# Summing the linear state over two token tiles in PSUM, and issuing it inside a value burst

## The chip, the cores and the metric

One core of one Trainium2 chip runs the whole program. The metric is device time in microseconds of that core; lower is better. Repeated runs of one kernel here spread over 0.5 to 2 us (0.1 to 0.4%), and the change is worth about as much or less, so most of this study reads stretches of the trace and not whole times.

## The reference, cut to what matters

Two attention blocks over the same x (2048 tokens, 1024 wide, 32 heads of 32) are mixed by a gate per token. Block A is linear attention, block B a local one with 8 positions at a dilation of 2.

```python
# block A
phi = lambda t: jnp.where(t > 0, t + 1, jnp.exp(t)) + 1e-6
pq, pk = phi(q), phi(k)
kv = jnp.einsum("bhsd,bhse->bhde", pk, v)      # the linear state
z  = jnp.einsum("bhsd->bhd", pk)               # its denominator part
num = jnp.einsum("bhqd,bhde->bhqe", pq, kv)
den = jnp.einsum("bhqd,bhd->bhq", pq, z)[..., None] + 1e-6
a = (num / den) @ wo_A
# block B: softmax over 8 earlier positions, times V, @ wo_B
g = sigmoid((x * gate_w).sum(-1, keepdims=True))
out = g * a + (1 - g) * b
```

## The kernel before

The program is a list of operations with reads and writes. A list scheduler in the kernel's own build step orders them for each engine by estimated times, and emits semaphore waits. TensorE does dense projections (128x512 matmuls in groups of 8, 1.73 us a group), and between them three kinds of short bursts of small matmuls: scores (S) and values (PV) of the local part, and the linear state (kv), one burst for each of 16 token tiles. A column of ones beside V (in az, the moving operand; pk is the stationary one) gives z as a 33rd column.

```python
vr = Ring([... "v%d" % i ... for i in range(3)])     # V of the local part, three deep
pk = Ring([... for i in range(2)])                   # phi(k) of a token tile
az = Ring([... for i in range(2)])                   # V of a token tile and ones
# ... cut ...
            def values():
                def each(e):        # 64 matmuls, 57 rows x 33 columns, 64x64 tiles
                    # ... cut ...
                P.op("pe", each, 0.55, mode="c", reads=[vt.all(), E.all()], writes=[s.iv for s in SO], name="PV")
                # ... cut: reciprocal and product on VectorE, store ...
# ... cut ...
        def slot(rate):             # called once for each dense group
            slot_n[0] += 1
            while later and later[0][0] <= slot_n[0]:
                later.pop(0)[1]()
            while states and states[0][0] <= slot_n[0]:
                states.pop(0)[1]()
            # ... cut ...
        def state(t, pkt, azt):
            bank = main.next()

            def fn(e):
                last = None
                for s in range(8):
                    for c in range(4):
                        h = 16 * (s // 4) + 4 * c + s % 4
                        last = e.matmul(bank.ap()[32 * c:32 * c + 32, s * 33:s * 33 + 33], pkt[:, h * 32:(h + 1) * 32], azt[:, h, :],
                                        start=True, stop=True, tile_position=(0, 32 * c))
                return last
            P.op("pe", fn, 0.22, mode="c", reads=[pkt.all(), azt.all()], writes=[bank.iv], name="kv")
            # VectorE: kva = bank (first tile) or kva + bank
# ... cut ...
                if r == 3:
                    states.append((slot_n[0] + 4, lambda t=t, pkt=pkt, azt=azt: state(t, pkt, azt)))
                slot(FILL)
# after the last tile, on VectorE: kvb and kvT (the state, transposed, for fold),
# and 16 small copies of z for the denominator:
        for c in range(4):
            for r in range(4):
                k = 4 * (c % 2) + r
                P.op("dve", lambda e, ...: e.tensor_copy(zsel[32 * r:32 * r + 32, c:8:4, k:k + 1], kva[32 * c:32 * c + 32, r:8:4, 32:33]), 0.1, ...)
# fold(): 16 matmuls of 32 rows x 512 into four banks: the state times wo_A, four times
# over(u): 8 matmuls for the denominators of 512 tokens (den), Ln and Exp on ScalarE,
#   then out to HBM and back as a broadcast (rc_hbm, rb), then 8 products on VectorE:
            for c in range(4):
                P.op("sp", ...dma_start(rc_hbm[...], R[...]), 0.5, ..., lat=0.5)
            # ... cut ...
                P.op("dve", lambda e, B=B, dst=dst: e.tensor_tensor(dst, dst, B[:, :], ALU.mult), 0.65, reads=[reg, B.all()], writes=[reg])
```

Of the kernel before, what the change touches and what calls it, by code (L numbers as in the profile page):

```python
# [7 lines left out]
ALU = mybir.AluOpType  # L8
AX = mybir.AxisListType
BF16 = mybir.dt.bfloat16  # L10
F32 = mybir.dt.float32
# [3 lines left out]
H = 32  # L15
# [1100 lines left out]
def build_kernel(nc, A_x, A_wqkv, A_wo, B_x, B_wqkv, B_wo, gate_w, out):  # L1116
# [67 lines left out]
    qd = Ring([SB([128, 8, 2, 114], BF16, "qd%d" % i, at=pq0.lo + 4096 * i) for i in range(2)])  # L1184
    par = SB([128, 2], F32, "par")
    eps = SB([128, 1], F32, "eps")
    gwb = SB([128, 1024], BF16, "gwb")
    gt = SB([128, NT], F32, "gt")
    g = SB([128, NT], F32, "g")
    gm = SB([128, NT], F32, "gm")  # L1190
# [2 lines left out]
    kva = SB([128, 8, 33], F32, "kva")  # L1193
    mx4 = SB([128, 4], F32, "mx4")
    mx1 = SB([1, 4], F32, "mx1")
    flag = SB([1, 1], I32, "flag")
    warm = SB([128, 512], BF16, "warm")
    er = Ring([SB([128, 512], BF16, "e%d" % i) for i in range(3)])

    ph = base[0]  # L1200
# [3 lines left out]
    Er = Ring([SB([128, 32 * 57], BF16, "E%d" % i) for i in range(2)])  # L1204
    ot = Ring([SB([128, 1024], BF16, "ot%d" % i) for i in range(2)])
    rs = Ring([SB([128, 16], F32, "rs%d" % i) for i in range(4)])
    vr = Ring([SB([128, 33 * H], BF16, "v%d" % i) for i in range(3)])
    mtmp = [SB([128, 2, 57], BF16, "mt%d" % i, at=vr.t[2].lo + 256 * i) for i in range(2)]
    base[0] = max(base[0], top_)
    kvT = SB([128, 256], BF16, "kvT")  # L1210
    RAr = Ring([SB([128, 512], F32, "ra%d" % i, at=t.lo) for i, t in enumerate((Er.t[0], Er.t[1]))])
    RBr = Ring([SB([128, 512], F32, "rb%d" % i, at=kT.lo + 2048 * i) for i in range(12)])
    mxr = SB([1, 4, 128], F32, "mxr", at=vr.t[2].lo)

    ph = base[0]
    mx = [SB([128, 1024], BF16, "mx%d" % i, at=ph + 2048 * i) for i in range(2)]
    pk = Ring([SB([128, 1024], BF16, "pk%d" % i) for i in range(2)])
    az = Ring([SB([128, H, 33], BF16, "az%d" % i) for i in range(2)])
    xn = Ring([SB([128, 1024], BF16, "xn%d" % i, at=az.t[i].lo) for i in range(2)])
    top_ = base[0]  # L1220
    base[0] = ph
# [12 lines left out]
    dps = lambda n: 0.14 + n / 960.0  # L1234

    def plan(seen):

        P = Prog(nc, nc.alloc_semaphore)
# [167 lines left out]
        SO = banks[4:8]  # L1406
# [37 lines left out]
        def rest(e_, qs, nq, t0, k0, m, vt, Q, s_fn):  # L1444
            P.op("pe", s_fn, 0.46, mode="r", reads=[kT.part((0, 8), (t0 + k0[0], t0 + k0[1] + 64)), Q.all()], writes=[s.iv for s in SO], name="S")
            E, _ = Er.next()
            P.op("act", lambda e: e.activation(E[:, 0:32 * nq].rearrange("p (j q) -> p j q", j=4), ps[:, 4:8, 0:8 * nq], ACT.Exp), act(32 * nq),  # L1447
                 reads=[s.iv for s in SO], writes=[E.all()])
            ev = lambda: E[:, 0:32 * nq].rearrange("p (g q) -> p g q", g=16)
            P.op("dve", lambda e: e.tensor_tensor(ev(), ev(), m[:, :, :].rearrange("p r q -> p (r q)")[:, None, :].to_broadcast([128, 16, 2 * nq]), ALU.mult),  # L1450
                 0.15 + 32 * nq / 1920.0, reads=[E.all(), m.all()], writes=[E.all()])

            def values():

                def each(e):
                    for i in range(16):
                        for w in range(2):
                            hd = 16 * w + i
                            for h in range(2):
                                c = 33 * (i % 8)  # L1460
                                g_ = place(hd)
                                last = e.matmul(SO[2 * h + i // 8].ap(c, c + 33)[64 * w:64 * w + nq, :], E[64 * h:64 * h + 64, g_ * nq:(g_ + 1) * nq],  # L1462
                                                vt[64 * h:64 * h + 64, hd * 33:hd * 33 + 33], start=True, stop=True, tile_position=(64 * h, 64 * w))
                    return last
                P.op("pe", each, 0.55, mode="c", reads=[vt.all(), E.all()], writes=[s.iv for s in SO], name="PV")
                o, os_ = ot.next()
                for h in range(2):
                    r, _ = rs.next()
                    bv = lambda h=h: ps[:, 4 + 2 * h:6 + 2 * h, 0:264].rearrange("p k (i c) -> p k i c", c=33)
                    two = [SO[2 * h].iv, SO[2 * h + 1].iv]  # L1470
                    P.op("dve", lambda e, r=r, bv=bv: e.reciprocal(r[:, :].rearrange("p (k i) -> p k i", k=2), bv()[:, :, :, 32:33].rearrange("p k i c -> p k (i c)")), 0.2,  # L1471
                         reads=two, writes=[r.all()])
                    P.op("dve", lambda e, r=r, bv=bv, h=h: e.tensor_tensor(  # L1473
                        o[:, 512 * h:512 * h + 512].rearrange("p (k i c) -> p k i c", k=2, c=32), bv()[:, :, :, 0:32],
                        r[:, :].rearrange("p (k i) -> p k i", k=2)[:, :, :, None].to_broadcast([128, 2, 8, 32]), ALU.mult), dps(512),
                        reads=two + [r.all()], writes=[o.part((512 * h, 512 * h + 512))])
                q0 = t0 + qs
                for w, (r0, r1) in [(w, r_) for w in range(2) for r_ in ((0, 48), (48, nq))]:
                    P.op("sp", lambda e, w=w, r0=r0, r1=r1: e.dma_start(
                        oB_hbm[q0:q0 + 2 * nq, 512 * w:512 * w + 512].rearrange("(h q) f -> q h f", h=2)[r0:r1], o[64 * w + r0:64 * w + r1, :].rearrange("p (h f) -> p h f", h=2)), 0.5,  # L1480
                        reads=[o.all()], writes=[[("O%d_%d" % (w, r0), q0, q0 + 2 * nq, None)]], chan="oo%d_%d_%d" % (os_, w, r0), lat=0.3)
                while rows[0] < NT and q0 + 2 * nq >= 128 * (rows[0] + 1):
                    t, rows[0] = rows[0], rows[0] + 1
                    P.op("sp", lambda e, t=t: e.dma_start_transpose(qT[:, :, t * 128:(t + 1) * 128], oB_hbm[t * 128:(t + 1) * 128, :]), 1.5,
                         reads=[[("O%d_%d" % (w, r0), t * 128, (t + 1) * 128, None)] for w in range(2) for r0 in (0, 48)], writes=[qT.part((0, 8), (t * 128, (t + 1) * 128))], chan="ot%d" % t, lat=1.3)
            after(PVLAG, values)
# [6 lines left out]
        def slot(rate):  # L1493
            slot_n[0] += 1
            while later and later[0][0] <= slot_n[0]:
                later.pop(0)[1]()
            while states and states[0][0] <= slot_n[0]:
                states.pop(0)[1]()
            pace[0] = min(pace[0] + rate, 1.0) if todo else 0.0
            if todo and pace[0] >= 1.0:  # L1500
                pace[0] -= 1.0
                fill(*todo.pop(0))
# [33 lines left out]
        for z in az.t:  # L1536
            P.op("pool", lambda e, z=z: e.memset(z[:, :, 32:33], 1.0), 0.2, writes=[z.part((0, H), (32, 33))])

        def state(t, pkt, azt):
            bank = main.next()  # L1540

            def fn(e):
                last = None
                for s in range(8):
                    for c in range(4):
                        h = 16 * (s // 4) + 4 * c + s % 4
                        last = e.matmul(bank.ap()[32 * c:32 * c + 32, s * 33:s * 33 + 33], pkt[:, h * 32:(h + 1) * 32], azt[:, h, :],  # L1547
                                        start=True, stop=True, tile_position=(0, 32 * c))
                return last
            P.op("pe", fn, 0.22, mode="c", reads=[pkt.all(), azt.all()], writes=[bank.iv], name="kv")  # L1550
            src = lambda: bank.ap(0, 264).rearrange("p (i c) -> p i c", c=33)
            if t == 0:
                P.op("dve", lambda e: e.tensor_copy(kva[:, :, :], src()), dps(264), reads=[bank.iv], writes=[kva.all()])
            else:
                P.op("dve", lambda e: e.tensor_tensor(kva[:, :, :], src(), kva[:, :, :], ALU.add), dps(264), reads=[bank.iv, kva.all()], writes=[kva.all()])

        for t in range(NT):
            pkt, _ = pk.next()
            azt, _ = az.next()
            xs, xr = x_tile(t)  # L1560
            for r in range(4):
                bank = main.next()
                w, wr = w_half((3, 0)[r // 2], r % 2)
                group(bank, xs, w, [xr, wr])
                if r < 2:
                    phi(bank, pkt[:, r * 512:(r + 1) * 512], pkt.part((r * 512, (r + 1) * 512)))
                else:
                    hh = (r - 2) * 16
                    dst = azt[:, hh:hh + 16, 0:32]
                    src = lambda bank=bank: bank.ap().rearrange("p (h d) -> p h d", d=32)  # L1570
                    reg = azt.part((hh, hh + 16), (0, 33))
                    move(dst, src, 512, bank, reg)
                if r == 3:
                    states.append((slot_n[0] + 4, lambda t=t, pkt=pkt, azt=azt: state(t, pkt, azt)))
                slot(FILL)
        while todo or later or states:
            slot(1.0)
# [222 lines left out]
```

## Time and profile before

| before | |
|---|---|
| time, median of 3 runs (of the later sets of 6 to 11 runs) | 488.56 us (medians 488.48 to 488.70) |
| profiled span, TensorE busy | 486.2 us, 98% |
| dense 128x512 matmul, start to start | 0.216 us |
| state bursts | 16 of 32 matmuls; 11 beside a value burst, 5 alone |
| state, cost on TensorE (worked out below) | 5.5 us |

First the page's span, its busy times, and the shares of the chain of work that ended last. PE is the matmuls, PEld the weight loads beside them.

```profile
span 486.2 us, 10107 instructions
...
PE 474.9 (98%) x4336; PEld 222.2 (46%) x4403; DVE 288.4 (59%) x557; ACT 139.0 (29%) x225; POOL 5.5 (1%) x34
...
PE 95%; DVE 2%; issue 1%; DMA 1%; SPq 0%; ACT 0%; DVEq 0%
```

The kernel is bound by TensorE from end to end. The list of its waits (columns: who waited for whom, us in total, times, longest) confirms it:

```profile
PE ps_all L1333 <- issue: 3.2, 20, 0.2
PE ps_all L1372 <- DVE warm L1282: 1.3, 1, 1.3
PE ps_all L1333 <- DMA xT<-in_A_x_dram: 0.8, 2, 0.6
PE ps_all L1333 <- DVE rs L1471: 0.5, 3, 0.2
PE ps_all L1333 <- ACT e L1340: 0.2, 1, 0.2
```

The 20 waits of 0.16 us for "issue" and the short ones for DVE and ACT are not waits. They stand before dense lines of 7, 15 or 23 matmuls where groups of 8 would make 8, 16 or 24: the first record of the group is missing.

Next the timeline of PE, merged (columns: start, length, line, operation, operands, count, and the idle time before). L1333 is dense, L1439 scores, L1462 values, L1547 the state.

```profile
199.49 0.60 PE L1439 MATMUL ps_all<-qd,kT 64*64 64x114 bf16 x32
200.03 1.90 PE L1333 MATMUL ps_all<-w,xT 128*128 128x512 bf16 x7
201.85 0.38 PE L1547 MATMUL ps_all<-az,pk 128*32 128x33 bf16 x32
202.17 3.63 PE L1333 MATMUL ps_all<-w,xT 128*128 128x512 bf16 x15
205.73 0.68 PE L1462 MATMUL ps_all<-v,E 64*57 64x33 bf16 x64
206.34 0.38 PE L1547 MATMUL ps_all<-az,pk 128*32 128x33 bf16 x32
206.88 3.40 PE L1333 MATMUL ps_all<-w,xT 128*128 128x512 bf16 x15 [0.16 <-issue]
```

A matmul's own length is modelled (177 ns for one of the state, the next starts 0 to 29 ns later), so lines overlap, and costs have to be taken from starts. The state burst at 201.85 us stands alone; the one at 206.34 us stands after a value burst. From the starts of the single matmuls in the trace:

- from the last dense start to the first small one 0.309 us, where the next dense matmul would come after 0.216 us;
- 32 starts of the state within 0.201 us (the line's 0.38 less the 0.18 of its last matmul), and 0.110 us from the last to what follows;
- 0.112 us from the last value start to the first state start.

So a burst alone costs 0.309 - 0.216 + 0.201 + 0.110 + 0.010 (the first dense step after it is 0.226 us) = 0.41 us, and one beside a value burst 0.31 us; 11 x 0.31 + 5 x 0.41 = 5.5 us.

Last, four lines that mark stretches: the first score burst, the first and second fold (L1599 in this kernel), and the 16 dense matmuls between them. They come from three windows of the timeline; the first line is cut by its window (12 of the 32 matmuls).

```profile
129.15 0.35 PE L1439 MATMUL ps_all<-qd,kT 64*64 64x114 bf16 x12
...
317.85 0.43 PE L1599 MATMUL ps_all<-w,kvT 32*32 32x512 bf16 x16
318.22 3.63 PE L1333 MATMUL ps_all<-xT,w 128*128 128x512 bf16 x16
321.91 0.44 PE L1599 MATMUL ps_all<-w,kvT 32*32 32x512 bf16 x16
```

First score burst to first fold: 317.85 - 129.15 = 188.70 us; all state bursts lie in it. The second fold starts 0.443 us after the last dense start before it, where an unhindered step is 0.309 us: a small wait of 0.13 us that was easy to overlook.

### The profile page before, as it was taken

The numbers are of one execution on the slowest core, as the hardware profiler recorded it, in microseconds if no ns is written. First come the engines' busy times: TensorE is split into PE (matmuls) and PEld (weight loads), VectorE is DVE, ScalarE is ACT, GpSimd is POOL, SyncE is SP. The second block draws the span as 40 slices with busy tenths as digits, with TensorE's granted clock in tenths as the row PEclk, the third lists the DMA queues.
The fourth block names the chain that finished last, engine by engine and source line by source line (L and its number), as shares of the span: only waits on it lengthen the run. The fifth ranks groups of instructions, "written<-read, shape, count | busy, mean of one in ns | idle before, by whom it ended". The sixth has DMA issues, their size and how long they took to land.

```text
span 486.2 us, 10107 instructions
## 1 busy us (share of the span) xinstructions
PE 474.9 (98%) x4336; PEld 222.2 (46%) x4403; DVE 288.4 (59%) x557; ACT 139.0 (29%) x225; POOL 5.5 (1%) x34
## 2 busy tenths in 40 slices
PE   8999999999999999999999999999999999999997
PEld 3444444444444444444444544444444444444443
DVE  2112336899788888575666656596865735434444
ACT  2111111214322233324534333455423322010000
POOL 4000000000000000000000000000000000000000
PEclk9999999999999999999999999999999999999999
DMA  8999992222014459423312322822674316101212
GB/s 221 225 208 309 357 361 63 85 89 87 2 43 142 106 153 233 99 77 84 77 44 65 98 55 48 200 51 41 160 190 98 99 17 179 43 24 44 88 67 89
DMA packets 72951, 57.39 MB, mean 118 GB/s; under 512 B 37953, under 2 KB 60865, under 8 KB 72898
## 3 DMA queue, kind: packets, MB, share of 16 engines
q1 hardware_dynamic: 72210, 56.07, 43.1%
q8 instruction: 36, 0.59, 0.5%
q10 hardware_dynamic: 688, 0.59, 0.4%
q14 instruction: 17, 0.14, 0.1%
HBM read 34.49 MB, written 13.76 MB: 99 GB/s over the span
## 4 chain that ended last, share of the span: by engine, by line
PE 95%; DVE 2%; issue 1%; DMA 1%; SPq 0%; ACT 0%; DVEq 0%
PE ps_all L1333 78%; PE ps_all L1675 11%; PE ps_all L1462 2%; PE ps_all L1439 2%; DMA xT<-in_A_x_dram 1%; PE ps_all L1547 1%; DVE zsel L1589 1%; PE ps_all L1626 0%; DVE pq L1346 0%; SPq L1307 0%; PE ps_all L1599 0%; SPq L1312 0%; DVE rs L1471 0%; DVE e L1344 0%; ACT e L1340 0%
## 5 line engine op out<-in xcount | busy, mean ns | idle before, releaser
L1333 PE MATMUL ps_all<-w,xT 128*128 128x512 bf16 x921 | 209.1, 379 | 4.6 <-issue 1.9
L1333 PE MATMUL ps_all<-xT,w 128*128 128x512 bf16 x747 | 168.3, 379 | 2.0 <-issue 1.3
L1333 PEld LDWEIGHTS ps_all<-w,xT 128*128 128x128 bf16 x960 | 91.1, 98 | 109.6 <-DMA xT<-in_A_x_dram 1.8
L1333 PEld LDWEIGHTS ps_all<-xT,w 128*128 128x128 bf16 x768 | 73.7, 98 | 89.0 <-issue 1.8
L1675 PE MATMUL ps_all<-w,qT 128*128 128x512 bf16 (+1 forms) x259 | 55.3, 372 | 0.3
L1675 PEld LDWEIGHTS ps_all<-w,qT 128*128 128x128 bf16 x264 | 25.8, 98 | 29.7
L1364 DVE CAST vst<-ps_all 128x512 bf16<-128x512 f32 x15 | 10.4, 694 | 43.1 <-PE ps_all L1333 43.1
L1447 ACT ACTIVATE E<-ps_all 128x1824 bf16<-128x1824 f32 (+1 forms) x18 | 30.4, 1687 | 13.4 <-PE ps_all L1439 13.4
L1344 DVE TENSOR_SCALAR e<-e 128x512 bf16<-128x512 bf16 x64 | 17.9, 283 | 26.6 <-ACT e L1342 15.6
L1679 DVE SCALAR_TENSOR_TENSOR o<-ps_all,gm,xT 128x512 bf16<-128x512 f32 (+1 forms) x25 | 18.1, 729 | 23.1 <-PE ps_all L1675 22.9
L1342 ACT ACTIVATE e<-ps_all 128x512 bf16<-128x512 f32 x32 | 19.1, 597 | 42.8 <-PE ps_all L1333 42.8
L1340 ACT ACTIVATE e<-ps_all 128x512 bf16<-128x512 f32 x32 | 19.1, 597 | 36.1 <-PE ps_all L1333 35.3
L1294 DVE TENSOR_TENSOR mx<-mx,kT 128x1024 bf16<-128x1024 bf16 x32 | 20.7, 686 | 9.3 <-ACT kT L1365 9.2
L1294 DVE TENSOR_TENSOR mx<-mx,qT 128x1024 bf16<-128x1024 bf16 x32 | 20.8, 686 | 6.6 <-ACT qT L1368 6.6
L1365 ACT ACTIVATE az<-ps_all 128x512 bf16<-128x512 f32 x22 | 13.2, 599 | 38.3 <-PE ps_all L1333 38.3
L1365 ACT ACTIVATE vst<-ps_all 128x512 bf16<-128x512 f32 x17 | 10.2, 599 | 47.5 <-PE ps_all L1333 47.5
L1473 DVE TENSOR_TENSOR ot<-ps_all,rs 128x512 bf16<-128x512 f32 x36 | 23.6, 683 | 0.2 <-DVE rs L1471 0.2
L1450 DVE TENSOR_TENSOR E<-E,msk 128x1824 bf16<-128x1824 bf16 (+1 forms) x18 | 19.9, 1103 | 5.8 <-ACT E L1447 5.2
L1346 DVE SCALAR_TENSOR_TENSOR pk<-ps_all,e 128x512 bf16<-128x512 f32 x32 | 21.9, 687 | 0.6
L1365 ACT ACTIVATE kT<-ps_all 128x512 bf16<-128x512 f32 x17 | 10.1, 597 | 39.8 <-PE ps_all L1333 39.8
L1368 ACT ACTIVATE qT<-ps_all 128x512 bf16<-128x512 f32 x17 | 10.1, 597 | 39.0 <-PE ps_all L1333 38.9
L1642 DVE TENSOR_TENSOR xT<-xT,rb 128x512 bf16<-128x512 bf16 x24 | 16.3, 688 | 8.5 <-DMA rb<-rc_hbm 8.4
(72 smaller groups left out, 259.1 us busy)
## 6 DMA issues: line engine op xcount, KB each, us to landing
rb<-rc_hbm SPq DMA_DIRECT2D x32, 256.0 KB, 5.0
w<-in_A_wqkv_dram SPq DMA_DIRECT2D x6, 1024.0 KB, 8.6
v<-vB_hbm SPq DMA_DIRECT2D x36, 132.0 KB, 3.0
vB_hbm<-vst SPq DMA_DIRECT2D x32, 132.0 KB, 6.2
w<-in_B_wqkv_dram SPq DMA_DIRECT2D x4, 1024.0 KB, 8.6
xn<-in_A_x_dram SPq DMA_DIRECT2D x16, 256.0 KB, 2.8
out_dram<-o SPq DMA_DIRECT2D x15, 256.0 KB, 2.1
oB_hbm<-ot SPq DMA_DIRECT2D x36, 96.0 KB, 2.1
```

The costliest lines, as they stand in the source:

```text
L1294: P.op("dve", lambda e, m=m, op=op: e.tensor_tensor(m[:, 0:n], m[:, 0:n], src, op), 0.08 + n / 1920.0, reads=[m.all(), reg], writes=[m.all()],
L1333: last = e.matmul(bank.ap(), lhs(dc), rhs(dc), start=(dc == 0), stop=(dc == 7))
L1340: P.op("act", lambda e: e.activation(e_[:, :], bank.ap(), ACT.Exp), act(512), reads=[bank.iv], writes=[e_.all()])
L1342: P.op("act", lambda e: e.activation(e_[:, :], bank.ap(), ACT.Exp, accum_out=qe[:, col:col + 1]), act(512) + 0.1, reads=[bank.iv], writes= ...
L1344: P.op("dve", lambda e: e.tensor_scalar(e_[:, :], e_[:, :], 1.0, 1e-6, op0=ALU.min, op1=ALU.add), 0.25, reads=[e_.all()], writes=[e_.all()])
L1346: P.op("dve", lambda e: e.scalar_tensor_tensor(out=dst, in0=bank.ap(), scalar=0.0, in1=e_[:, :], op0=ALU.max, op1=ALU.add), dps(512), read ...
L1365: fa = lambda e: e.activation(dst, src(), ACT.Copy)
L1447: P.op("act", lambda e: e.activation(E[:, 0:32 * nq].rearrange("p (j q) -> p j q", j=4), ps[:, 4:8, 0:8 * nq], ACT.Exp), act(32 * nq), rea ...
L1450: P.op("dve", lambda e: e.tensor_tensor(ev(), ev(), m[:, :, :].rearrange("p r q -> p (r q)")[:, None, :].to_broadcast([128, 16, 2 * nq]), ...
L1473: P.op("dve", lambda e, r=r, bv=bv, h=h: e.tensor_tensor(o[:, 512 * h:512 * h + 512].rearrange("p (k i c) -> p k i c", k=2, c=32), bv()[:, ...
L1675: last = e.matmul(bank.ap(0, f1 - f0), qT[:, dc, t * 128:(t + 1) * 128], ws[3][:, dc, f0:f1], start=(dc == 0), stop=(dc == 7))
L1679: P.op("dve", lambda e, bank=bank, o_=o_, t=t, n=n, i0=i0, i1=i1, tgt=tgt, c0=c0: e.scalar_tensor_tensor(out=o_[:, i0 * 128:i1 * 128].rear ...
```

## The change

Intent: two token tiles are summed in PSUM, so that 16 bursts of 32 become 8 of 64 with fewer changes of tile form and half the adds on VectorE; and the burst is made part of the value burst's operation, so that it cannot stand alone. The rings of phi(k) and V deepen from 2 to 4 to hold two pairs; to pay for the space, V of the local part goes from three to two deep, the gate weights and the warm-up data (gwb, warm) lie in the new buffers of phi(k), and mask and end scratch (mtmp, mxr) move to another tile.

```diff
-    vr = Ring([SB([128, 33 * H], BF16, "v%d" % i) for i in range(3)])
-    mtmp = [SB([128, 2, 57], BF16, "mt%d" % i, at=vr.t[2].lo + 256 * i) for i in range(2)]
+    vr = Ring([SB([128, 33 * H], BF16, "v%d" % i) for i in range(2)])
+    mtmp = [SB([128, 2, 57], BF16, "mt%d" % i, at=ot.t[1].lo + 256 * i) for i in range(2)]
 ... (mxr moves the same way; warm and gwb lose places of their own)
-    pk = Ring([SB([128, 1024], BF16, "pk%d" % i) for i in range(2)])
-    az = Ring([SB([128, H, 33], BF16, "az%d" % i) for i in range(2)])
+    pk = Ring([SB([128, 1024], BF16, "pk%d" % i) for i in range(4)])
+    az = Ring([SB([128, H, 33], BF16, "az%d" % i) for i in range(4)])
+    warm = SB([128, 512], BF16, "warm", at=pk.t[2].lo)
+    gwb = SB([128, 1024], BF16, "gwb", at=pk.t[3].lo)
 ...
-                P.op("pe", each, 0.55, mode="c", reads=[vt.all(), E.all()], writes=[s.iv for s in SO], name="PV")
+                fns, rd, wr, add = [each], [vt.all(), E.all()], [s.iv for s in SO], None
+                if len(states) > 1 and states[1][0] <= slot_n[0]:
+                    fn, more, bank, add = state([states.pop(0)[1] for _ in range(2)])
+                    fns, rd, wr = fns + [fn], rd + more, wr + [bank.iv]
+                P.op("pe", lambda e: [f(e) for f in fns][-1], 0.55 + 0.5 * (len(fns) - 1), mode="c", reads=rd, writes=wr, name=...)
+                if add is not None:
+                    add()
 ...
-            while states and states[0][0] <= slot_n[0]:
-                states.pop(0)[1]()
+            if len(states) > 1 and states[1][0] + 2 <= slot_n[0] and not later:
+                fn, rd, bank, add = state([states.pop(0)[1] for _ in range(2)])
+                P.op("pe", fn, 0.42, mode="c", reads=rd, writes=[bank.iv], name="kv")
+                add()
 ... (state takes two tiles, its add is emitted by the caller)
                 for s in range(8):
-                    for c in range(4):
-                        ... start=True, stop=True, tile_position=(0, 32 * c))
+                    for i, (t, pkt, azt) in enumerate(two):
+                        for c in range(4):
+                            ... start=(i == 0), stop=(i == len(two) - 1), tile_position=(0, 32 * c))
 ...
-                    states.append((slot_n[0] + 4, lambda ...))
+                    states.append((slot_n[0] + 1, (t, pkt, azt)))
```

More of the change, by code (lines that the diff above doesn't have):

```diff
@@ L1186, in build_kernel @@
     eps = SB([128, 1], F32, "eps")
-    gwb = SB([128, 1024], BF16, "gwb")
     gt = SB([128, NT], F32, "gt")
@@ L1196, in build_kernel @@
     flag = SB([1, 1], I32, "flag")
-    warm = SB([128, 512], BF16, "warm")
     er = Ring([SB([128, 512], BF16, "e%d" % i) for i in range(3)])
@@ L1212, in build_kernel @@
     RBr = Ring([SB([128, 512], F32, "rb%d" % i, at=kT.lo + 2048 * i) for i in range(12)])
-    mxr = SB([1, 4, 128], F32, "mxr", at=vr.t[2].lo)
+    mxr = SB([1, 4, 128], F32, "mxr", at=ot.t[1].lo)
     ph = base[0]
     mx = [SB([128, 1024], BF16, "mx%d" % i, at=ph + 2048 * i) for i in range(2)]
-    pk = Ring([SB([128, 1024], BF16, "pk%d" % i) for i in range(2)])
-    az = Ring([SB([128, H, 33], BF16, "az%d" % i) for i in range(2)])
+    pk = Ring([SB([128, 1024], BF16, "pk%d" % i) for i in range(4)])
+    az = Ring([SB([128, H, 33], BF16, "az%d" % i) for i in range(4)])
+    warm = SB([128, 512], BF16, "warm", at=pk.t[2].lo)
+    gwb = SB([128, 1024], BF16, "gwb", at=pk.t[3].lo)
     xn = Ring([SB([128, 1024], BF16, "xn%d" % i, at=az.t[i].lo) for i in range(2)])
@@ L1464, in each @@
                     return last
-                P.op("pe", each, 0.55, mode="c", reads=[vt.all(), E.all()], writes=[s.iv for s in SO], name="PV")
+                fns, rd, wr, add = [each], [vt.all(), E.all()], [s.iv for s in SO], None
+                if len(states) > 1 and states[1][0] <= slot_n[0]:
+                    fn, more, bank, add = state([states.pop(0)[1] for _ in range(2)])
+                    fns, rd, wr = fns + [fn], rd + more, wr + [bank.iv]
+                P.op("pe", lambda e: [f(e) for f in fns][-1], 0.55 + 0.5 * (len(fns) - 1), mode="c", reads=rd, writes=wr, name="PV" if add is None else "PV+kv")
+                if add is not None:
+                    add()
                 o, os_ = ot.next()
@@ L1537, in plan, with state, add @@
             P.op("pool", lambda e, z=z: e.memset(z[:, :, 32:33], 1.0), 0.2, writes=[z.part((0, H), (32, 33))])
-        def state(t, pkt, azt):
+        def state(two):
             bank = main.next()
             def fn(e):
-                last = None
                 for s in range(8):
-                    for c in range(4):
-                        h = 16 * (s // 4) + 4 * c + s % 4
-                        last = e.matmul(bank.ap()[32 * c:32 * c + 32, s * 33:s * 33 + 33], pkt[:, h * 32:(h + 1) * 32], azt[:, h, :],
-                                        start=True, stop=True, tile_position=(0, 32 * c))
-                return last
-            P.op("pe", fn, 0.22, mode="c", reads=[pkt.all(), azt.all()], writes=[bank.iv], name="kv")
-            src = lambda: bank.ap(0, 264).rearrange("p (i c) -> p i c", c=33)
-            if t == 0:
-                P.op("dve", lambda e: e.tensor_copy(kva[:, :, :], src()), dps(264), reads=[bank.iv], writes=[kva.all()])
-            else:
-                P.op("dve", lambda e: e.tensor_tensor(kva[:, :, :], src(), kva[:, :, :], ALU.add), dps(264), reads=[bank.iv, kva.all()], writes=[kva.all()])
+                    for i, (t, pkt, azt) in enumerate(two):
+                        for c in range(4):
+                            h = 16 * (s // 4) + 4 * c + s % 4
+                            last = e.matmul(bank.ap()[32 * c:32 * c + 32, s * 33:s * 33 + 33], pkt[:, h * 32:(h + 1) * 32], azt[:, h, :],
+                                            start=(i == 0), stop=(i == len(two) - 1), tile_position=(0, 32 * c))
+                return last
+            def add():
+                src = lambda: bank.ap(0, 264).rearrange("p (i c) -> p i c", c=33)
+                if two[0][0] == 0:
+                    P.op("dve", lambda e: e.tensor_copy(kva[:, :, :], src()), dps(264), reads=[bank.iv], writes=[kva.all()])
+                else:
+                    P.op("dve", lambda e: e.tensor_tensor(kva[:, :, :], src(), kva[:, :, :], ALU.add), dps(264), reads=[bank.iv, kva.all()], writes=[kva.all()])
+            return fn, [x.all() for _, p, a in two for x in (p, a)], bank, add
         for t in range(NT):
@@ L1573, in plan @@
                 if r == 3:
-                    states.append((slot_n[0] + 4, lambda t=t, pkt=pkt, azt=azt: state(t, pkt, azt)))
+                    states.append((slot_n[0] + 1, (t, pkt, azt)))
                 slot(FILL)
```

## The prediction

> **What bounds the kernel now.** TensorE. The page shows PE busy 98% of 486.2 us; the chain of waits is 95% PE; the list of PE's waits adds up to about 6 us, mostly at the start (1.3 and 0.8 us) or "issue" slivers of 0.16 us that come from missing matmul records. The clock is 0.999. VectorE (59%) and ScalarE (29%) matter only if PE comes to wait for them.
>
> **What the state costs now.** The timeline of PE from 191 to 318 us shows 16 bursts of 32 small matmuls. By the starts of single matmuls, dense 128x512 ones follow each other every 0.216 us; from the last dense start to the first of a small burst it is 0.309 us (0.093 us lost to the change of tile form); inside the state burst 32 starts take 0.201 us, 6.5 ns each; from its last start to what follows 0.110 us; from a value burst's last start to the state burst 0.112 us. The Trainium skill, "TensorEngine Tiling (Array Packing)", Key Properties, says that changing the tiling mode drains the engine; the steps of 0.09 to 0.11 us are its price here, paid between value burst (64-row tiles) and state burst (128-row tiles) too. So a state burst alone among dense matmuls costs about 0.41 us, one beside a value burst 0.31 us. Eleven of 16 already stand beside a value burst: 11 x 0.31 + 5 x 0.41 = 5.5 us.
>
> **What the change does.** The changed instruction order has 8 state bursts of 64 matmuls, 7 right after a value burst and 1 alone before the fold; matmuls and weight loads stay 512. At 6.5 ns a start a burst takes 0.41 us, plus 0.112 us for the switch: 7 x 0.52 + 1 x 0.62 = 4.3 us. Saved: about 1.2 us, all on the critical path. VectorE loses 8 of 16 adds (about 0.4 us each), off the critical path: worth nothing directly.
>
> **What it adds.** (a) The second matmul of a pair adds into columns that the first wrote 4 starts (26 ns) earlier. The skill, "TensorE: Matmul & The Clock Gate", section "Wait — 56ns, not 53.3ns?", gives a floor of about 25 ns from start to start; here each column tile starts every 26 ns, so I expect no further stall. (b) Value and state bursts become one operation: it waits for both tiles' evictions, and normalisation starts 0.5 us later. A dense group (1.73 us) or more lies before the burst and two before the next score burst: 0 to 0.4 us of new waits in all. (c) V two deep: a load waits for the value burst two before, some 10 us ahead of need, against 3 us to landing: no wait. (d) Memory overlaps (gate weights, warm-up data, masks): no wait; start and tail stay.
>
> **Predicted.** 488.56 - 1.2 + 0.2 = 487.5 us, range 486.5 to 488.7. Chances: faster by over 2% 0.01, within 2% 0.97, slower by over 2% 0.02.
>
> **What would show it.** 8 bursts of 64 starts in 0.41 us; 7 directly after a value burst; state total 4.3 us; no new line in PE's waits above 0.3 us; 8 adds into kva; dense matmuls still at 0.216 us.
>
> **What would make it wrong.** Adding in PSUM at 26 ns distance stalls (64 starts taking 0.6 us or more: gain gone); value bursts waiting for the az eviction just before; reordered VectorE/ScalarE queues making dense groups wait for a bank.

## The result, and the profile after

| | before | after |
|---|---|---|
| time, median of 6 runs each in alternating rounds | 488.48 us (488.10 to 489.16) | 488.06 us (487.89 to 488.53) |
| ratio after to before, 95% interval | | 0.9992 (0.9979 to 1.0005): the same |
| first score burst to first fold | 188.70 us | 188.09 us |
| first fold to first denominator burst | 14.11 us | 14.54 us |
| first denominator burst to last dense start | 150.92 us | 151.37 us |
| profiled span | 486.2 us | 486.3 us |

A ratio is the mean time of one kernel's fast runs over the mean of the other's fast runs of the same rounds, so it is not quite the ratio of the medians quoted. Here the median fell by 0.4 us and the interval includes 1. The three stretches of the table explain the span: 0.61 us won, then 0.43 and 0.45 us lost, and the start, which differs by 0.2 us between the two profiles. Over all twelve profiles the first score burst begins between 128.84 and 129.85 us, whatever the kernel: what happens in the first 16 us moves a single span by up to a microsecond, more than the change does. In that time TensorE waits for loads, and its first matmuls, 6 to 13 of them by profile, follow each other at 0.43 us and not at 0.216.

The same page lines and the waits of the changed kernel. The state is now L1555, the fold L1609, the denominators L1636.

```profile
span 486.3 us, 10100 instructions
...
PE 474.7 (98%) x4339; PEld 222.8 (46%) x4403; DVE 284.0 (58%) x544; ACT 142.3 (29%) x230; POOL 5.8 (1%) x36
...
PE 91%; DMA 3%; DVE 2%; issue 1%; SPq 1%; ACT 1%; ACTq 0%
```

```profile
PE ps_all L1333 <- issue: 3.5, 22, 0.2
PE ps_all L1372 <- DVE warm L1282: 1.3, 1, 1.3
PE ps_all L1333 <- DMA xT<-in_A_x_dram: 0.6, 2, 0.4
PE ps_all L1609 <- DVE pq L1346: 0.5, 1, 0.5
PE ps_all L1636 <- DVE xT L1346: 0.2, 1, 0.2
```

Two entries are new: the fold and a denominator burst wait for VectorE's feature map (L1346). The timeline of PE around a paired burst:

```profile
194.82 1.67 PE L1333 MATMUL ps_all<-w,xT 128*128 128x512 bf16 x7
196.43 0.68 PE L1462 MATMUL ps_all<-v,E 64*57 64x33 bf16 x64
197.04 0.67 PE L1555 MATMUL ps_all<-az,pk 128*32 128x33 bf16 x64
197.86 3.40 PE L1333 MATMUL ps_all<-w,xT 128*128 128x512 bf16 x15 [0.16 <-issue]
```

The burst follows the value burst as planned, but 64 starts take 0.67 - 0.19 = 0.48 us, not 0.41. In the starts of single matmuls the first 32 still come within 0.20 us (steps of 3, 4, 3, 15 ns); from about the 33rd on every step is 8.4 ns, the same for all eight bursts. The whole state costs 7 x 0.595 + 0.70 = 4.9 us (beside a value burst 0.112 + 0.479 and 0.004 on leaving; alone 0.309 - 0.216 + 0.479 + 0.120 + 0.010), 0.6 us less than before. The stretch from first score burst to first fold, marked again by lines from windows of the timeline, agrees: 317.04 - 128.95 = 188.09 us.

```profile
128.95 0.24 PE L1439 MATMUL ps_all<-qd,kT 64*64 64x114 bf16 x4
...
317.04 0.43 PE L1609 MATMUL ps_all<-w,kvT 32*32 32x512 bf16 x16
317.41 3.63 PE L1333 MATMUL ps_all<-xT,w 128*128 128x512 bf16 x16
321.54 0.44 PE L1609 MATMUL ps_all<-w,kvT 32*32 32x512 bf16 x16 [0.50 <-DVE pq L1346]
```

The second fold now starts 0.880 us after the last dense start before it: 0.57 us of waiting, 0.44 us more than before. What VectorE did in that time is in its own timeline of the changed kernel (L1564 the last add of the state, L1599 here the copies into zsel, L1346 the feature map that frees a bank):

```profile
313.64 0.43 DVE L1564 TENSOR_TENSOR kva<-ps_all,kva 128x264 f32<-128x264 f32 x1 [2.58 <-PE ps_all L1555]
...
315.24 2.73 DVE L1599 CAST zsel<-kva 32x2 bf16<-32x2 f32 x14
318.00 0.69 DVE L1346 SCALAR_TENSOR_TENSOR pq<-ps_all,e 128x512 bf16<-128x512 f32 x1
...
320.80 0.68 DVE L1346 SCALAR_TENSOR_TENSOR pq<-ps_all,e 128x512 bf16<-128x512 f32 x1
```

Fourteen tiny copies hold VectorE for 2.73 us, and the feature maps and evictions behind them come late; the fold at 321.54 us starts when the last of these feature maps is done. The same copies and the same feature map in the kernel before, where the copies are L1589:

```profile
316.01 2.73 DVE L1589 CAST zsel<-kva 32x2 bf16<-32x2 f32 x14
...
321.18 0.68 DVE L1346 SCALAR_TENSOR_TENSOR pq<-ps_all,e 128x512 bf16<-128x512 f32 x1
```

### The profile page after: what moved, and what is told of

It is laid out like the page before. It is cut to its first block, busy times and chain, and to the rows that moved or that the text cites. A ratio compares the mean times of both kernels' runs of the same rounds, so it can differ in the third digit from the quotient of the medians.

```text
span 486.3 us, 10100 instructions
## 1 busy us (share of the span) xinstructions
PE 474.7 (98%) x4339; PEld 222.8 (46%) x4403; DVE 284.0 (58%) x544; ACT 142.3 (29%) x230; POOL 5.8 (1%) x36
## 4 chain that ended last, share of the span: by engine, by line
PE 91%; DMA 3%; DVE 2%; issue 1%; SPq 1%; ACT 1%; ACTq 0%
PE ps_all L1333 74%; PE ps_all L1685 11%; PE ps_all L1462 2%; PE ps_all L1439 2%; DMA rb<-rc_hbm 1%; PE ps_all L1555 1%; DMA xT<-in_A_x_dram 1%; DMA rc_hbm<-ra 1%; SPq L1649 1%; DVE zsel L1599 1%; DVE xT L1652 1%; DVE pq L1346 0%; PE ps_all L1636 0%; SPq L1307 0%; DVE xT L1346 0%
## 5 line engine op out<-in xcount | busy, mean ns | idle before, releaser
L1365 ACT ACTIVATE az<-ps_all 128x512 bf16<-128x512 f32 x22 | 13.2, 599 | 34.5 <-PE ps_all L1333 34.5
L1365 ACT ACTIVATE kT<-ps_all 128x512 bf16<-128x512 f32 x20 | 11.9, 596 | 38.2 <-PE ps_all L1333 38.2
L1346 DVE SCALAR_TENSOR_TENSOR pk<-ps_all,e 128x512 bf16<-128x512 f32 x32 | 21.9, 688 | 0.7
L1368 ACT ACTIVATE qT<-ps_all 128x512 bf16<-128x512 f32 x19 | 11.3, 597 | 37.4 <-PE ps_all L1333 37.3
L1652 DVE TENSOR_TENSOR xT<-xT,rb 128x512 bf16<-128x512 bf16 x24 | 16.4, 690 | 7.8 <-DMA rb<-rc_hbm 7.7
```

Source lines behind the costliest of these rows:

```text
L1346: P.op("dve", lambda e: e.scalar_tensor_tensor(out=dst, in0=bank.ap(), scalar=0.0, in1=e_[:, :], op0=ALU.max, op1=ALU.add), dps(512), read ...
L1365: fa = lambda e: e.activation(dst, src(), ACT.Copy)
```

## The experiments

Ten kernels were run, in three sets; each set shares the runs of the kernel before on one chip. One further build, the changed kernel with V of the local part back at three deep, did not fit: it goes over the partition's memory by 544 bytes. V is tested from the other side below.

### Is it the sum in PSUM that slows the long burst? (no_sum)

The changed kernel; both matmuls of a pair overwrite. Its output is wrong, which doesn't matter for the time.

```diff
-  start=(i == 0), stop=(i == len(two) - 1), tile_position=(0, 32 * c))
+  start=True, stop=True, tile_position=(0, 32 * c))
```

> The changed kernel, but both matmuls of a pair overwrite (no sum in PSUM), on purpose wrong: the state then holds only the odd tiles. Question: why do the 64 starts of a paired burst take 0.479 us and not the 0.408 us predicted. Theory A (instruction supply: about 32 pairs of weight load and matmul lie ready when a burst begins, the rest come at 8.4 ns each): nothing changes, 64 starts in 0.47 to 0.49 us, the first 32 in 0.20 us. Theory B (adding in PSUM 26 ns after the first write stalls): 64 starts in 0.40 to 0.42 us. Whole time as the changed kernel, within 0.7 us, under both (B would save 0.6 us).

Measured: the bursts take 0.480 to 0.483 us, as with the sum; one run, 488.45 us. The line of the same burst in its timeline:

```profile
197.81 0.67 PE L1555 MATMUL ps_all<-az,pk 128*32 128x33 bf16 x64
```

Theory B falls: adding 26 ns after the first write costs nothing that can be seen. As the program's order is that of the changed kernel, this profile also repeats its waits: 0.891 us before the second fold, and 0.711 us before a denominator burst.

### Does the slow part follow the count? (twice)

The pair's matmuls are issued twice over, tile by tile. In each pass only the first matmul of each column tile clears, and the later ones of the first token tile rely on cleared bits: this is an idiom that the Trainium skill, "PSUM — Partial Sum Buffer", The four PSUM rules, describes for groups that share a bank, and the correct result agrees with it.

```diff
-  for s in range(8):
-      for i, (t, pkt, azt) in enumerate(two):
+  for i, (t, pkt, azt) in [(i, x) for _ in range(2) for i, x in enumerate(two)]:
+      for s in range(8):
 ...
-  start=(i == 0), stop=(i == len(two) - 1), tile_position=(0, 32 * c))
+  start=(i == 0 and s == 0), stop=(i == len(two) - 1), tile_position=(0, 32 * c), skip_group_check=True)
```

> The changed kernel with each paired burst issued twice over (128 matmuls; tile by tile, first matmul of the bank clears, so the result stays right). Theory A (instruction supply): the first 32 starts in 0.20 us, the other 96 at 8.4 ns: 128 starts in 1.00 to 1.03 us, no break where the adding tile begins or ends. Theory B (adding stalls): the cadence goes fast, slow, fast, slow with the tiles, 128 starts in about 0.95 us or less, and the third group of 32 back at 6.5 ns. Cost under A: 8 bursts x 0.54 us = 4.3 us more than the changed kernel.

Measured: correct, one run, 501.49 us, 13 us more and not 4.3. Half of the bursts (4 of 8) take 1.013 us, as theory A says, with no return to the fast cadence in the third 32. The other four stop once each in the middle:

```profile
197.43 0.93 PE L1555 MATMUL ps_all<-az,pk 128*32 128x33 bf16 x95
200.63 0.38 PE L1555 MATMUL ps_all<-az,pk 128*32 128x33 bf16 x33 [2.27 <-issue]
...
244.28 1.20 PE L1555 MATMUL ps_all<-az,pk 128*32 128x33 bf16 x128
```

The first two lines are one burst that stops for 2.3 us, the last a burst that does not. The stretch from first score burst to first fold is 13.2 us longer than in the changed kernel: 8 x (1.013 - 0.479) = 4.3 us of theory A, 7.3 us in the four stops, and 1.7 us after the second stopped burst. There the dense group does not stop: seven of its steps take 0.427 us and two 0.29 and 0.35 us, where 0.216 is usual, and the granted clock is 0.54 from 223.5 to 227.2 us; after the two other stops of 2 us and more nothing of the kind is seen. In the four stops TensorE waits for nothing that the profile shows. A shortage of instructions is what fits: the page counts 39 packets of 16.4 KB (0.64 MB) on the queue that it calls "instruction", against 36 in the kernels before and after (the 1024 added instructions would fill four), and one packet is, by estimate, 256 instructions at the 64 bytes that the Trainium skill, "TensorE: Matmul & The Clock Gate", Step-by-step, gives for a MATMUL (taking the same for a weight load): just the 128 weight loads and 128 matmuls of one such burst. That it is the fetch that stops the engine is argued from this, not shown.

The supply theory fits the same page's statement (table at its top) that TensorE's queue is 64 deep: 32 pairs of weight load and matmul. The traces show exactly 32 starts at 6.5 ns and then 8.4 ns a pair, and after three of the four stops the next 32 starts are fast again (0.21 to 0.22 us). Value bursts are alike: their first 36 to 44 starts come at about 7.3 ns (after one gap of 41 ns), the rest at 8.4. But the theory is not shown, and in its plain form it does not account for the count. Seven of the changed kernel's bursts begin 0.112 us after the slow end of a value burst, in which time only 13 pairs would arrive at 8.4 ns each, and the eighth comes after dense matmuls; all eight turn slow after the same 32 starts. In the run alone, below, the first burst also stands right behind a value burst, and it is slow from its first start (64 starts in 0.556 us). What is shown is that neither the sum, nor the tile, nor the place in the bank makes the second half slow; what sets 32 and 8.4 ns stays open.

### Does the sum in PSUM matter at all? (two_banks)

Each tile of a pair gets a bank of its own, and VectorE adds both, so 16 adds again.

```diff
-  bank = main.next()
+  bank = [main.next() for _ in two]
 ...
-  e.matmul(bank.ap()[...], ..., start=(i == 0), stop=(i == len(two) - 1), ...)
+  e.matmul(bank[i].ap()[...], ..., start=True, stop=True, ...)
 ... (the add runs over both banks)
```

> The changed kernel, but each tile of a pair goes to a bank of its own and VectorE adds both (16 adds again, as before). If the sum in PSUM is worth nothing by itself and only where the bursts stand counts: bursts of 64 in 0.47 to 0.49 us, PE cost of the state 4.9 us as in the changed kernel, time within 0.5 us of it. If two banks of the four are too many to hold: new waits of PE of 1 us or more in the stage from 190 to 318 us. If the eight adds removed from VectorE matter: slower by 1 us or more.

Measured: correct, 487.97 us, ratio to before 0.9990 (0.9973 to 1.0007), the same as the changed kernel's 0.9992. Bursts of 0.480 us; first score burst to first fold 188.26 us, 0.17 us more than the changed kernel. Summing in PSUM, taken alone, is worth 0.2 us or less here; the saving lies in pairing and placing the bursts, which the next run takes apart. The whole time is no clean test of the sum, as the scheduler also moved the second fold behind one more dense group, where it does not wait (0.310 us step).

### Does the place matter? (alone)

Pairs summed in PSUM, but as operations of their own that the scheduler does not put beside value bursts.

```diff
-  if len(states) > 1 and states[1][0] <= slot_n[0]:            # in the value burst
+  if False:
 ...
-  if len(states) > 1 and states[1][0] + 2 <= slot_n[0] and not later:
+  if len(states) > 1 and states[1][0] <= slot_n[0]:
 ...
-  P.op("pe", fn, 0.42, mode="c", ...)
+  P.op("pe", fn, 0.42, mode="k", ...)
```

> The changed kernel's paired sums, but not inside the value burst: each pair is an operation of its own and most of them (5 of 8) stand among dense matmuls, 3 next to another small burst. If the place next to a value burst is what saves (0.60 us a pair beside, 0.70 us alone): state cost 3 x 0.60 + 5 x 0.70 = 5.3 us, 0.4 us more than the changed kernel and level with before (5.5 us). If pairing saves by itself (one switch for two tiles): 4.9 us or less.

Measured: correct, 489.00 us, ratio 1.0004 (0.9987 to 1.0022). First score burst to first fold is 189.19 us: 1.10 us more than the changed kernel, where 0.4 was expected, and 0.5 us more than before. The state bursts account for 0.5 us of it (5 alone at 0.70 us; two of the eight took 0.54 and 0.56 us from first to last start, and not 0.48). Another 0.53 us is a score burst that stopped:

```profile
197.50 0.74 PE L1555 MATMUL ps_all<-az,pk 128*32 128x33 bf16 x64
198.40 1.67 PE L1333 MATMUL ps_all<-w,xT 128*128 128x512 bf16 x7 [0.16 <-issue]
200.01 0.49 PE L1439 MATMUL ps_all<-qd,kT 64*64 64x114 bf16 x23
200.81 0.34 PE L1439 MATMUL ps_all<-qd,kT 64*64 64x114 bf16 x9 [0.30 <-issue]
```

A value burst, a state burst, one dense group and a score burst stand within 4 us here, and the last breaks off for "issue", as the bursts of twice did. The order of the changed kernel leaves two dense groups there, and neither its profile nor the others with its order show such a stop. Without the stop the stretch would be some 188.7 us, level with before: pairing without the place wins nothing that can be told here. The reverse, single tiles all beside another burst, was not run; an estimate from the steps of the kernel before (0.112 + 0.201, less 0.004 on leaving) is 16 x 0.309 = 4.9 us, as much as the changed kernel's state costs.

### Do the copies into zsel cause the wait at the fold? (zsel_late and before_zsel_late)

A lower priority for the 16 copies, and a planned cost of 0.2 instead of 0.1 us (they take 0.16); once on the changed kernel, once on the kernel before.

```diff
-  ...kva[32 * c:32 * c + 32, r:8:4, 32:33]), 0.1, reads=[kva.all()], writes=[zsel.all()])
+  ...kva[32 * c:32 * c + 32, r:8:4, 32:33]), 0.2, reads=[kva.all()], writes=[zsel.all()], prio=1000 + len(P.ops) + 50)
```

> The changed kernel with one edit: the 16 small copies into zsel (about 3 us of VectorE in a row, right after the last add) get a lower priority, so that the feature map and the evictions of the fold go first. Theory: the second fold waits 0.57 us (0.880 instead of 0.309 us from the dense start before it) for banks that VectorE frees late because of those copies. Then that step is back at 0.31 us and the time is 0.4 to 0.6 us lower than the changed kernel's, unless the denominator matmuls take the loss over (they wait on reciprocals' DMA). Rival: the fold waits for the last state add itself; then the wait stays.

> The kernel before with the same edit of the zsel copies. It waited 0.13 us at the second fold (0.443 against 0.309 us). Theory: 0.1 us lower, not to be told from noise in the time; the step itself goes to 0.31 us. So the loss at the fold belongs for the most part to the changed kernel, where the state ends 0.6 us earlier but VectorE does not.

Measured on the changed kernel: 487.49 us, ratio to before 0.9981 (0.9967 to 0.9995). TensorE's order is unchanged, and the fold follows at once (0.309 us from the last dense start):

```profile
317.98 3.63 PE L1333 MATMUL ps_all<-xT,w 128*128 128x512 bf16 x16
321.54 0.43 PE L1609 MATMUL ps_all<-w,kvT 32*32 32x512 bf16 x16
```

First fold to first denominator burst falls from 14.54 to 13.97 us. On the kernel before, 488.47 us, ratio 0.9996 (0.9983 to 1.0010), and the same stretch falls from 14.11 to 13.97 us. So the copies cost the kernel before 0.13 us and the changed kernel 0.57 us. Both have the same distance of two dense groups between last state burst and first fold. In both, the second fold needs the bank that the third feature map after the copies frees. In the changed kernel TensorE reaches the first fold 0.81 us earlier (317.04 against 317.85 us) and the copies end 0.77 us earlier, but that feature map ends only 0.38 us earlier (321.48 against 321.86 us), because the plan put two evictions of the fold before it and not one. The rival, that the fold waits for the last add, falls.

### Why do the denominators wait? (rb_late, before_v2)

In the changed kernel's profile two denominator bursts wait 0.15 and 0.30 us for a feature map that stands in VectorE's queue behind products which wait for a DMA. A lower priority for those products:

```diff
-  ...e.tensor_tensor(dst, dst, B[:, :], ALU.mult), 0.65, reads=[reg, B.all()], writes=[reg])
+  ...e.tensor_tensor(dst, dst, B[:, :], ALU.mult), 0.65, reads=[reg, B.all()], writes=[reg], prio=1000 + len(P.ops) + 40)
```

> The changed kernel with one edit: the VectorE products with the reciprocals, which wait for a DMA, get a lower priority than the feature map of the next chunk. Theory: the denominator matmuls of the second and third chunk waited 0.15 and 0.30 us because the feature map stood in VectorE's queue behind a product that waited for its DMA. Then both steps are back at 0.31 us and the time is 0.2 to 0.5 us lower. Rival: the DMAs land late whatever the order, and the waits only move to the output matmuls of the linear part: no gain.

Measured: 487.60 us, ratio 0.9978 (0.9963 to 0.9992), but not for the reason expected. The scheduler also moved denominator bursts on TensorE (8, 12 and 15 dense groups apart instead of 9, 10 and 16), one still waits (0.651 us step), and from first score burst to last dense start the profile has 353.92 us, as much as the changed kernel's 354.00. The edit did not isolate what it was to test, and its better time stays unexplained by its profile, which was taken of the slowest of its five runs (488.44 us; the others took 487.29 to 487.64).

The other half of the answer comes from the kernel before with V of the local part two deep:

```diff
-  vr = Ring([SB([128, 33 * H], BF16, "v%d" % i) for i in range(3)])
+  vr = Ring([SB([128, 33 * H], BF16, "v%d" % i) for i in range(2)])
 ... (mtmp and mxr move into ot.t[1], as in the change)
```

> The kernel before with V of the local part two deep (and the mask scratch moved with it), nothing else. Theory: no wait on V in PE's list, the bursts of PE as before, time within 0.3 us of before. Rival: loads of V that wait for a value burst hold up the queue of loads behind them: value or score bursts later by 0.3 us or more in the stage from 129 to 311 us.

Measured: correct, 488.80 us, ratio 1.0011 (0.9987 to 1.0035); first score burst to first fold 188.69 us (188.70 before). V two deep costs nothing there. But this kernel, which has no part of the new state, shows denominator steps of 0.687 and 0.408 us, and the kernel before with late copies 0.664 and 0.672 us, while the first profile of before has 0.309 us in all. The waits are there with and without the change and differ from profile to profile. The 0.45 us that the last stretch lost is therefore no effect of the change that could be shown.

### Both losses mended, with the change and without (best2, before_best2)

The late copies, and in the plan a slower way out for the reciprocals, so that the scheduler itself puts the products later. TensorE's order stays as it was in each kernel.

```diff
-  chan="rco%d_%d" % (rs, c), lat=0.5)
+  chan="rco%d_%d" % (rs, c), lat=1.25)
 ... (and the edit of zsel_late)
```

> The changed kernel with the zsel copies late and, in the plan, the reciprocals' DMA taken as 3 us slower, so that the products which wait for it stand behind one more feature map in VectorE's queue; TensorE's order is unchanged. Theory: fold step 0.31 us, all four denominator steps 0.31 us in this and every run, state cost 4.9 us: 0.6 us (state) + 0.1 us (fold) + 0.1 to 0.7 us (denominators, which differ from run to run of the kernel before) below before, so about 487.3 us, ratio 0.997 to 0.9985. Rival: the denominator waits come from the DMA itself, not from the order in the queue: steps of 0.4 us and more are still seen.

> The kernel before with the same two edits (zsel copies late, reciprocals' DMA taken as slower). Theory: fold and denominator steps at 0.31 us, state cost 5.5 us as before; so what is left between this and the run above is the change itself, 0.6 us (from the first score burst to the last dense start), and the time is 0 to 0.6 us below before. Rival: if the change also costs or saves elsewhere, the two differ by more or less than 0.5 to 0.7 us in that stretch.

| | with the change (best2) | without (before_best2) |
|---|---|---|
| time, median of 6 | 487.37 us | 488.12 us |
| ratio to before | 0.9971 (0.9958 to 0.9985) | 0.9981 (0.9968 to 0.9994) |
| fold and denominator steps | all 0.31 us | all 0.31 us |
| first score burst to last dense start | 352.96 us | 353.59 us |

The waits of TensorE in best2 are down to the start; these two lines are the whole list:

```profile
PE ps_all L1333 <- DMA xT<-in_A_x_dram: 1.4, 2, 1.1
PE ps_all L1372 <- DVE warm L1282: 1.3, 1, 1.3
```

With nothing else in the way the change is worth 353.59 - 352.96 = 0.63 us on TensorE, in one profile of each. The medians, from the same rounds, differ by 0.75 us, but the two intervals overlap, so the times alone do not separate the two. best2 is the fastest version by its median; it beats the kernel before by 0.3%. It was not timed in the same rounds as the changed kernel; in the traces it is 1.04 us shorter over this stretch (352.96 against 354.00). No denominator wait was seen in its one profile nor in that of before_best2; as the waits come and go, two profiles make it likely, not certain, that the new order removes them. The profile of zsel_late, which has only the first of the two edits, shows no denominator wait either and 352.99 us for the stretch, so what the second edit adds is not shown.

## Why the prediction was right or wrong

The time lay in the range (488.06 in 486.5 to 488.7) and "within 2%" was right. But the range also held the 488.56 us of no gain at all, so that the time fell into it says little: it was wide enough. The gain itself was mis-sized, and one loss was denied.

- **Bound by TensorE; 8 bursts, 7 after a value burst.** Right, by the timeline.
- **"At 6.5 ns a start a burst takes 0.41 us".** This is the term that was mis-sized. It measured 0.479 us: only the first 32 starts come at 6.5 ns, the rest at 8.4, for a reason that stays open. Eight times 0.07 is 0.56 us, so the state costs 4.9 us and not 4.3, and the saving is 0.6 us (0.61 in the pair of profiles, 0.63 with the other waits removed), not 1.2. Value bursts in the profile before already showed the slower second half, and it was not looked at.
- **The sum in PSUM does not stall.** Right: 0.480 us without the sum. The reason given, the floor of 25 ns from start to start, agreed with 26 ns for each column tile only in the first half of a burst; in the second the distance is 34 ns, set by something else.
- **Waits on evictions 0 to 0.4 us.** None at the bursts: stretch and burst costs agree to 0.01 us.
- **V two deep and shared memory cost nothing.** V is shown by before_v2. Shared scratch was not tested by itself; the start lies within the spread of all profiles.
- **"Start and tail stay"; VectorE's work is off the critical path.** Wrong at one place. For some 8 us after the last state burst VectorE is the engine that TensorE depends on, and the fold lost 0.44 us more than before to the copies there (zsel_late gives 0.57 back, before_zsel_late 0.13). That took most of what the state had won.
- **Where the rest went.** Predicted was a gain of 1.2 less 0.2 for waits, 1.0 us; measured 0.4 by the medians. By the traces 0.6 was won and 0.4 given back at the fold; the denominator waits and the start add or take up to a microsecond in one profile and belong to neither kernel.

## What to carry to other kernels

A short burst costs its changes of tile form, so count how many bursts already stand beside another before joining them: here 11 of 16 did, and joining two of those gained only 0.02 us (2 x 0.309 against 0.595 us), while moving one out of the dense stream gained 0.1. Do not extend the cadence of a short burst to a longer one; read the second half of the longest burst already in the trace. And when the bound engine gets ahead by half a microsecond, look for the next place where another engine sits in front of it: a row of tiny copies there can take the gain, and a lower priority for them gives it back.

## What the Trainium skill lacked or had wrong

- "TensorE: Matmul & The Clock Gate" gives the queue's depth of 64 but not what follows when a burst is longer: here 32 pairs of weight load and matmul at 6.5 ns, then 8.4 ns a pair, in the changed kernel's state bursts of 64 (0.479 us) and in unbroken ones of 128 (1.013 us). Whether the queue is the reason is not shown. Its floor of about 25 ns from start to start is met within one column tile in those first 32 starts (26 ns); for the 34 ns after them it has no figure.
- No page that I found tells that dense small matmuls without a branch can be held up by the supply of instructions (the point belongs to "Runtime: NRT & Kernel Launch", which describes the fetch). Bursts of 128 pairs stopped in 4 of 8 cases for 0.5 to 2.4 us with no wait that the profile shows, and a score burst soon after a value and a state burst lost 0.53 us. That the supply is the cause is argued from the instruction queue's packets of 16.4 KB, not shown.
- "TensorEngine Tiling (Array Packing)", Key Properties, says that changing the tiling mode drains the engine, without a figure. Here: 0.093 us going from dense to small tiles, about 0.11 us from value to state burst, 0.11 to 0.14 us back to dense.
- "PSUM — Partial Sum Buffer" does not say how soon a second matmul may add to a column without a stall. Here 26 ns after the first write costs nothing (0.479 against 0.480 us for 64 starts).
